# Attention and two feed-forward blocks in one kernel: other SBUF places for the matmul operands, a later normalisation, another prologue

## The chip, the core and the metric

One core of a Trainium2 chip runs the whole program. TensorE (PE, with its weight loads PEld), VectorE (DVE), ScalarE (ACT), GpSimd (POOL) and SyncE (SP) run side by side, each through its own instructions in order; they wait for each other on semaphores. SBUF is the working memory (128 partitions), PSUM holds what TensorE adds up. The metric is device time in microseconds (us).

## The reference

```python
x = attention(q, k, v, cap)              # 2 x 12 heads, 448 positions, head size 64
#   s = cap * tanh(q k^T / 8 / cap);  p = exp(s - max);  p v / (sum p + 1e-9)
x = x.transpose(0, 2, 1, 3).reshape(896, 768)
y = ((x @ w_a) * (x @ w_b)) @ w_out      # 768 -> 1536 -> 768
h = relu(y @ w_in)
out = (h * h) @ w_out2                   # 768 -> 2048 -> 768
```

The weights come in double precision, all else in single; the output is single.

## The kernel before

**Prologue.** Queries and keys of head pair 0, the number `cap`, pair 1 (`qk1`, into the third raw weight buffer) and the first unit of weights are loaded (lines 525 to 530). Eight matmuls on a small constant `warm` keep TensorE busy meanwhile. Then come the scores of pair 0, three DVE instructions that turn `cap` into the factor `c1`, and the tanh of pair 0 on ScalarE (lines 541 to 549).

**Attention.** A loop over 12 head pairs; one pass is a period. In a period `j`, TensorE computes the scores of pair `j+1` (`qk_main`, L52), their last 64 rows (`tails`, L58, into the PSUM tile `dn`), the products with `v` (L251, L286) and the column sums (L292, L294). ScalarE does tanh and exp. DVE adds up exp values (`presum`, L279 and L280), copies the results out of PSUM (`evac`: `ev` L298, `dv` L301) and normalises older pairs: `dv` goes through DMA into a shape with more partitions (`s8`, L304), is inverted (`recips`), written to DRAM (`dscr`, L328) and read back as a broadcast `rb` (`spread`, L335); `norm` (L342) multiplies `ev` by `rb`. `xhi` and `xlo` split the result into the two parts (high and low) that the products below take. `dv` has one buffer, and `dn` one bank: the next `tails` waits until `dv` has read `dn`.

**Weights.** A unit is six blocks of 128 x 128 weights (68 units). `conv(u, step)` turns the double-precision raw data of unit `u` into two parts in seven steps, which end in one of four buffers `whl0` to `whl3` (unit `u` uses number `u mod 4`). Steps 6 (L122 or L124) and 7 (L129) write the buffer. During attention the steps are spread over the periods by the table `CONV_AT`.

**Products.** `mm` (L184) multiplies a block with an operand tile: high part of the weights times low part of the operand (L189), low times high (L191), high times high (L193), each for two halves of 448 columns, so that a block is six matmuls and a unit 36, of one weight load (128 columns) and 448 streamed columns each. The operands are `x`, `g`, `y` and `h` (its last tile is `hlast`), one after another through the four matrix products; there are 2448 such matmuls, and a unit's weights are made three units ahead.

**Places.** In the built program the byte address in a partition, modulo 256, of each buffer's first byte in use is the following (`placed`, `HLAT` and the filler tiles set it; within a tile all parts lie at multiples of 256 bytes from its start, so a tile has one remainder):

| operand tiles | remainder | distance from `whl0` (at 0) | `whl1` (32) | `whl2` (64) | `whl3` (128) |
|---|---|---|---|---|---|
| `x` | 0 | 0 | 224 | 192 | 128 |
| `g` | 160 | 160 | 128 | 96 | 32 |
| `y` | 96 | 96 | 64 | 32 | 224 |
| `h` (tile at 224, data 48 bytes in) | 16 | 16 | 240 | 208 | 144 |
| `hlast` | 0 | 0 | 224 | 192 | 128 |

The distance is that of the operand behind the weights, modulo 256.

Of the kernel before, what the change touches and what calls it, by code (L numbers as in the profile page):

```python
# [37 lines left out]
HLAT = (0, 32, 64, 128)  # L38
# [9 lines left out]
def score(nc, banks, qk):  # L48
    for n in range(2 * NC):
        c, i = divmod(n, 2)  # L50
        r = slice(i * D, (i + 1) * D)
        nc.tensor.matmul(banks[n // NC][:, n % NC, :S], lhsT=qk[r, 1, c * P:(c + 1) * P], rhs=qk[r, 0], start=True, stop=True)  # L52


def score_tail(nc, out, qk):
    for i in range(2):
        r = slice(i * D, (i + 1) * D)
        nc.tensor.matmul(out[r, :S], lhsT=qk[r, 1, NM:], rhs=qk[r, 0], start=True, stop=True)  # L58
# [11 lines left out]
def placed(pool, name, n, gap, lead=0, room=0):  # L70
    if gap:
        pool.tile([P, gap // 4], F32, name=f"{name}gap")
    size = 2 * B * S
    tiles = [pool.tile([P, size + room // 4], F32R, name=f"{name}{i}")[:, lead // 4:lead // 4 + size] for i in range(n)]
    return [t.rearrange("p (t b s) -> p t b s", t=2, b=B) for t in tiles]


def body(ctx, tc, qk, v, wu, out, c1, cabs, guard, dscr, qk1, kept, bounded):
# [17 lines left out]
    cur = 0  # L96
    whl = []
    for i, a in enumerate(HLAT):
        if a - cur:
            wp.tile([P, (a - cur) // 4], F32, name=f"whlgap{i}")  # L100
        whl.append(wp.tile([P, 2, UC], F32R, name=f"whl{i}"))
        cur = a
# [98 lines left out]
    xhl = placed(xpool, "x", KD, 128)  # L201
# [35 lines left out]
    def qk_main(j):  # L237
        th = tht[j] = ap.tile([P, NT, S], F32, tag="th", name="th", bufs=1)
        sc = [ps.tile([P, NC, 512], F32, tag="sc", name="sc") for _ in range(2)]
        score(nc, sc, qkt[j])  # L240
# [3 lines left out]
    def tails(j):  # L244
        pvt[j] = pq[0].tile([P, 512], F32, tag="pv", name="pv")
        dnt[j] = pq[0].tile([P, 512], F32, tag="dn", name="dn")
        if j + 1 < NPAIR:
            score_tail(nc, dnt[j], qkt.pop(j + 1))
# [47 lines left out]
    def evac(j):  # L296
        ev = ap.tile([P, S], F32, tag="ev", name="ev", bufs=5)
# [9 lines left out]
    def finish(j):  # L307
# [8 lines left out]
        rb = ap.tile([P, S], F32, tag="rb", name="rb", bufs=2)  # L316
# [13 lines left out]
    def spread(j):  # L330
        if j < 0:
            return
        rb = ap.tile([P, S], F32, tag="rb", name="rb", bufs=2)
# [27 lines left out]
    for n in range(7):  # L361
        conv(0, n + 1, True)
# [15 lines left out]
    for j in range(last):  # L378
        qk_main(j + 1)
        presum(j)  # L380
        if j > 0:
# [7 lines left out]
        xhi(j - 4)  # L389
        xlo(j - 4)  # L390
        steps(j)
        norm(j - 3)
# [5 lines left out]
    spread(last - 2)  # L398
    xhi(last - 4)
# [38 lines left out]
    ghl = placed(gp, "g", NF1, 0)  # L438
    gp.tile([P, 16], F32, name="gback")
# [16 lines left out]
    yhl = placed(yp, "y", KD, 224)  # L456
# [10 lines left out]
    hhl = placed(hpool, "h", NF2 - 1, 0, 48, 256)  # L467
# [38 lines left out]
def tile_kernel(ctx, tc, qk, v, cap, wu, out):  # L506
# [12 lines left out]
    h_last = keep.tile([P, 2, B, S], F32R, name="hlast")  # L519
# [3 lines left out]
    with tc.manual_schedule():  # L523
        craw, cabs, c1, small, eps = (cp.tile([P, 1], F32, name=n) for n in ("craw", "cabs", "c1", "small", "eps"))
        qk0 = wk.tile([P, 2, S], F32, name="qk0")
# [85 lines left out]
```

## Time and profile before

| | |
|---|---|
| median of 3 runs | 599.25 us (598.66 to 599.28) |
| the profiled execution: its time | 599.35 us |
| its span, first to last instruction | 597.2 us |
| TensorE busy, share of the span | 585.3 us, 98% |
| VectorE busy | 389.8 us, 65% |
| ScalarE busy | 239.8 us, 40% |
| mean granted TensorE clock | 0.999 |

The profile is one execution. A busy TensorE row is a modelled span of pipelined matmuls, so its pace is read from start times, not from durations. All times below count from the first instruction; the time of the run has 2.15 us more than the span.

### The profile page before, as it was taken

How to read it: one execution, taken by the hardware profiler on the slowest of the kernel's cores; microseconds unless marked ns; L12 is line 12 of the kernel's file. 1: busy time of each engine (PE TensorE's matmuls, PEld its weight loads, DVE VectorE, ACT ScalarE, POOL GpSimd, SP SyncE). 2: the span in 40 equal slices, each digit the busy share in tenths (PEclk: the TensorE clock that was granted, in tenths of full speed). 3: DMA queues.
4: the chain of work that ended last, by engine and by line, in shares of the span. 5: the costliest groups of instructions: out<-in, count | busy, mean ns of one | idle time of the engine just before them, and what ended most of it. 6: DMA issues, size and time to landing. Idle time of an engine off the chain costs nothing.

```text
span 597.2 us, 7213 instructions
## 1 busy us (share of the span) xinstructions
PE 585.3 (98%) x2936; PEld 488.0 (82%) x2936; DVE 389.8 (65%) x525; ACT 239.8 (40%) x250; POOL 0.3 (0%) x5
## 2 busy tenths in 40 slices
PE   8899899999999999999999999999999999999996
PEld 2233236999999999999999999999999999999995
DVE  3778788788666666657555548787877686526400
ACT  6899790344333333322222224444444433212200
POOL 0000000000000000000000000000000000000000
PEclk9999999999999999999999999999999999999999
DMA  7455431244333333332333332332332335323001
GB/s 244 158 166 168 136 113 67 93 159 156 112 112 111 105 106 105 107 107 77 134 105 106 106 105 95 113 110 106 106 106 106 105 107 190 136 85 107 31 32 36
DMA packets 20549, 67.68 MB, mean 113 GB/s; under 512 B 6044, under 2 KB 9756, under 8 KB 20508
## 3 DMA queue, kind: packets, MB, share of 16 engines
q1 hardware_dynamic: 19356, 62.75, 31.0%
q10 hardware_dynamic: 1152, 4.39, 2.2%
q8 instruction: 25, 0.41, 0.3%
q14 instruction: 16, 0.13, 0.1%
HBM read 64.26 MB, written 2.79 MB: 112 GB/s over the span
## 4 chain that ended last, share of the span: by engine, by line
PE 93%; DMA 3%; DVE 2%; SPq 0%; issue 0%; ACT 0%; DVEq 0%
PE sc L189 19%; PE sc L191 19%; PE sc L193 19%; PE pd L193 9%; PE pd L191 9%; PE pd L189 9%; PE pv L286 4%; PE sc L52 3%; DMA raw<-in_wu_dram 1%; PE dn L292 1%; PE dn L58 1%; DMA s<-dv 1%; DMA dscr<-rc 1%; DMA rb<-dscr 0%; DVE sm L280 0%; DVE sm L279 0%
## 5 line engine op out<-in xcount | busy, mean ns | idle before, releaser
L124 ACT ACTIVATE whl<-nar 128x768 fp32r<-128x768 f32 x65 | 55.1, 847 | 181.7 <-DVE nar L149 154.8
L129 DVE TENSOR_TENSOR whl<-nar,whl 128x768 fp32r<-128x768 f32 x68 | 65.1, 958 | 40.0 <-ACT whl L124 40.0
L147 DVE SCALAR_TENSOR_TENSOR nar<-raw,nar 128x768 int32<-128x768 int32 x68 | 65.2, 958 | 2.3
L149 DVE SCALAR_TENSOR_TENSOR nar<-raw,nar 128x768 int32<-128x768 int32 x68 | 64.9, 955 | 1.4
L141 ACT ACTIVATE nar<-nar 128x768 f32<-128x768 f32 x65 | 54.3, 835 | 20.9 <-DVE nar L134 20.9
L189 PE MATMUL sc<-x,whl 128*128 128x448 f32 x192 | 56.7, 366 | 0.0
L191 PE MATMUL sc<-x,whl 128*128 128x448 f32 x192 | 56.6, 365 | 0.0
L193 PE MATMUL sc<-x,whl 128*128 128x448 f32 x192 | 56.6, 366 | 0.0
L145 DVE TENSOR_SCALAR nar<-nar 128x768 int32<-128x768 int32 x68 | 37.6, 552 | 18.0 <-ACT nar L141 17.6
L134 DVE TENSOR_SCALAR nar<-raw 128x768 f32<-128x768 f32 x68 | 37.6, 553 | 3.4 <-DMA raw<-in_wu_dram 3.4
L189 PEld LDWEIGHTS sc<-x,whl 128*128 128x128 f32 x192 | 36.0, 188 | 4.4 <-issue 1.4
L193 PEld LDWEIGHTS sc<-x,whl 128*128 128x128 f32 x192 | 36.0, 188 | 3.1
L191 PEld LDWEIGHTS sc<-x,whl 128*128 128x128 f32 x192 | 36.0, 188 | 3.0
L189 PE MATMUL sc<-y,whl 128*128 128x448 f32 x132 | 37.6, 366 | 0.0
L191 PE MATMUL sc<-y,whl 128*128 128x448 f32 x132 | 37.6, 365 | 0.0
L193 PE MATMUL sc<-y,whl 128*128 128x448 f32 x132 | 37.5, 365 | 0.0
L193 PE MATMUL sc<-h,whl 128*128 128x448 f32 x120 | 36.6, 366 | 0.0
L189 PE MATMUL sc<-h,whl 128*128 128x448 f32 x120 | 36.6, 366 | 0.0
L191 PE MATMUL sc<-h,whl 128*128 128x448 f32 x120 | 36.6, 366 | 0.0
L273 ACT ACTIVATE pe<-th,cabs 128x3136 f32<-128x3136 f32 x12 | 34.9, 2910 | 0.4
L242 ACT ACTIVATE th<-sc,c 128x1344 f32<-128x1344 f32 x22 | 29.1, 1375 | 7.7 <-PE sc L52 7.7
L286 PE MATMUL pv<-pe,vt 128*64 128x448 f32 x144 | 29.7, 548 | 0.0
(126 smaller groups left out, 996.9 us busy)
## 6 DMA issues: line engine op xcount, KB each, us to landing
raw<-in_wu_dram SPq DMA_DIRECT2D x63, 768.0 KB, 4.2
qk<-in_qk_dram SPq DMA_DIRECT2D x10, 448.0 KB, 4.4
raw<-in_wu_dram ACTq DMA_DIRECT2D x5, 768.0 KB, 5.5
vt<-in_v_dram SPq DMA_DIRECT2D x12, 224.0 KB, 4.6
rb<-dscr SPq DMA_DIRECT2D x22, 112.0 KB, 2.8
out_dram<-th SPq DMA_DIRECT2D x5, 448.0 KB
raw<-in_qk_dram SPq DMA_DIRECT2D x1, 448.0 KB, 6.5
s<-dv SPq DMA_DIRECT2D x22, 3.5 KB
```

The costliest lines, as they stand in the source:

```text
L124: nc.scalar.activation(out=hl[:, 0], in_=nar_t[u], func=AF.Copy)
L129: nc.vector.tensor_tensor(out=hl[:, 1], in0=nar_t.pop(u), in1=f32(hl[:, 0]), op=ALU.subtract)
L134: nc.vector.tensor_scalar(out=t, in0=raw_t[u][:, :, 1].bitcast(F32), scalar1=WTOP, scalar2=-WTOP, op0=ALU.min, op1=ALU.max)
L141: nc.scalar.activation(out=t, in_=t, func=AF.Copy, scale=2.0 ** -112)
L145: nc.vector.tensor_scalar(out=t, in0=t, scalar1=3, scalar2=None, op0=ALU.logical_shift_left)
L147: nc.vector.scalar_tensor_tensor(out=t, in0=r[:, :, 0], scalar=29, in1=t, op0=ALU.logical_shift_right, op1=ALU.bitwise_or)
L149: nc.vector.scalar_tensor_tensor(out=t, in0=r[:, :, 1], scalar=-(1 << 31), in1=t, op0=ALU.bitwise_and, op1=ALU.bitwise_or)
L189: nc.tensor.matmul(o[:, b, :S], lhsT=hi, rhs=m[:, 1, b], start=first, stop=False)
L191: nc.tensor.matmul(o[:, b, :S], lhsT=lo, rhs=m[:, 0, b], start=False, stop=False)
L193: nc.tensor.matmul(o[:, b, :S], lhsT=hi, rhs=m[:, 0, b], start=False, stop=last)
L273: nc.scalar.activation(out=pe, in_=th, func=AF.Exp, scale=cabs)
L286: nc.tensor.matmul(pvt[j][(1 - i) * D:(2 - i) * D, :S], lhsT=vt[:, n], rhs=pe[:, n], start=False, stop=c == NC - 1)
```

## The change

Four things change. (1) The four weight buffers lie at remainder 0, and every operand tile (`x`, `g`, `y`, `h`, `hlast`) at remainder 160: one distance, 160 bytes modulo 256, for all 2448 matmuls. `HLAT` goes, and `placed` takes filler before and behind instead. (2) In the attention loop `xhi`, `xlo` and `norm` work on a pair that is one period older; `ev` and `rb` get one more buffer each, and the set that falls out of the loop stands behind it. (3) Steps 6 and 7 of unit 0 are done behind the first `presum` instead of ahead of the first exp. (4) In the prologue `cap` is loaded by GpSimd's queue, the keys of pair 0 in two pieces, the first unit of weights by ScalarE's queue; the scores go to three PSUM tiles instead of two, and the tanh in three pieces behind them.

```diff
-HLAT = (0, 32, 64, 128)
...
-def placed(pool, name, n, gap, lead=0, room=0):
-    if gap:
-        pool.tile([P, gap // 4], F32, name=f"{name}gap")
-    size = 2 * B * S
-    tiles = [pool.tile([P, size + room // 4], F32R, name=f"{name}{i}")[:, lead // 4:lead // 4 + size] for i in range(n)]
-    return [t.rearrange("p (t b s) -> p t b s", t=2, b=B) for t in tiles]
+def placed(pool, name, n, before=0, behind=0):
+    if before:
+        pool.tile([P, before // 4], F32, name=f"{name}before")
+    tiles = [pool.tile([P, 2, B, S], F32R, name=f"{name}{i}") for i in range(n)]
+    if behind:
+        pool.tile([P, behind // 4], F32, name=f"{name}behind")
+    return tiles
...
-    cur = 0
-    whl = []
-    for i, a in enumerate(HLAT):
-        if a - cur:
-            wp.tile([P, (a - cur) // 4], F32, name=f"whlgap{i}")
-        whl.append(wp.tile([P, 2, UC], F32R, name=f"whl{i}"))
-        cur = a
+    whl = [wp.tile([P, 2, UC], F32R, name=f"whl{i}") for i in range(HLB)]
...
-    xhl = placed(xpool, "x", KD, 128)
+    xhl = placed(xpool, "x", KD, before=160)
...
-        ev = ap.tile([P, S], F32, tag="ev", name="ev", bufs=5)
+        ev = ap.tile([P, S], F32, tag="ev", name="ev", bufs=6)
...
-        rb = ap.tile([P, S], F32, tag="rb", name="rb", bufs=2)
+        rb = ap.tile([P, S], F32, tag="rb", name="rb", bufs=3)
...
-    for n in range(7):
+    for n in range(5):
...
+        if j == 0:
+            conv(0, 6, True)
+            conv(0, 7, True)
...
-        xhi(j - 4)
-        xlo(j - 4)
+        xhi(j - 5)
+        xlo(j - 5)
         steps(j)
-        norm(j - 3)
+        norm(j - 4)
...
+    xhi(last - 5)
+    xlo(last - 5)
+    norm(last - 4)
...
-    ghl = placed(gp, "g", NF1, 0)
-    gp.tile([P, 16], F32, name="gback")
+    ghl = placed(gp, "g", NF1, behind=64)
...
-    yhl = placed(yp, "y", KD, 224)
+    yhl = placed(yp, "y", KD, before=160)
...
-    hhl = placed(hpool, "h", NF2 - 1, 0, 48, 256)
+    hhl = placed(hpool, "h", NF2 - 1, behind=64)
...
-    h_last = keep.tile([P, 2, B, S], F32R, name="hlast")
+    h_last = placed(keep, "hlast", 1, before=160, behind=96)[0]
...
-        qk0 = wk.tile([P, 2, S], F32, name="qk0")
-        nc.sync.dma_start(out=qk0[:, 0], in_=qk[0, :, 0])
-        nc.scalar.dma_start(out=qk0[:, 1], in_=qk[0, :, 1])
-        nc.sync.dma_start(out=craw, in_=cap.broadcast_to([P, 1]))
+        q0, ka, kb = (wk.tile([P, n], F32, name=m) for n, m in ((S, "q0"), (P, "ka"), (S - P, "kb")))
+        nc.gpsimd.dma_start(out=craw, in_=cap.broadcast_to([P, 1]))
+        nc.sync.dma_start(out=q0, in_=qk[0, :, 0])
+        nc.scalar.dma_start(out=ka, in_=qk[0, :, 1, :P])
+        nc.scalar.dma_start(out=kb, in_=qk[0, :, 1, P:])
         nc.sync.dma_start(out=qk1, in_=qk[1])
-        fetch(nc.sync, raws, wu, 0)
+        fetch(nc.scalar, raws, wu, 0)
...
-        sc = [wps.tile([P, NC, 512], F32, tag="sc", name="sc") for _ in range(2)]
+        sc = [wps.tile([P, 2, 512], F32, name=f"sc{c}", bufs=1) for c in range(NC)]
...
-        score(nc, sc, qk0)
-        score_tail(nc, tl, qk0)
-        for part in range(2):
-            nc.scalar.activation(out=th0[:, part * NC:(part + 1) * NC], in_=sc[part][:, :, :S], func=AF.Tanh, scale=c1)
+        k0 = [ka] + key_blocks(kb, P)
+        score(nc, [t[:, n, :S] for t in sc for n in range(2)], q0, k0)
+        score_tail(nc, tl, q0, k0[NC])
+        for c in range(NC):
+            nc.scalar.activation(out=th0[:, 2 * c:2 * c + 2], in_=sc[c][:, :, :S], func=AF.Tanh, scale=c1)
```

On DVE, at pair 0, before (rows of unit 0's conversion, `presum` of pair 0, unit 1's first steps):

```order
L147 SCALAR_TENSOR_TENSOR nar_171<-raw0_66,nar_171 128x768
L149 SCALAR_TENSOR_TENSOR nar_171<-raw0_66,nar_171 128x768
L122 CAST whl0_145<-nar_171 128x768
L129 TENSOR_TENSOR whl0_145<-nar_171,whl0_145 128x768
L556 TENSOR_SCALAR small_81<-small_81 128x1
L279 TENSOR_TENSOR sm_206<-pe_179 128x896
L280 TENSOR_TENSOR sm_206<-sm_206,pe_179 128x896
L134 TENSOR_SCALAR nar_219<-raw1_67 128x768
L139 TENSOR_SCALAR nar_219<-nar_219 128x768
```

and now:

```order
L145 SCALAR_TENSOR_TENSOR nar_175<-raw0_66,nar_175 128x768
L147 SCALAR_TENSOR_TENSOR nar_175<-raw0_66,nar_175 128x768
L562 TENSOR_SCALAR small_83<-small_83 128x1
L278 TENSOR_TENSOR sm_208<-pe_181 128x896
L279 TENSOR_TENSOR sm_208<-sm_208,pe_181 128x896
L120 CAST whl0_152<-nar_175 128x768
L127 TENSOR_TENSOR whl0_152<-nar_175,whl0_152 128x768
L132 TENSOR_SCALAR nar_223<-raw1_67 128x768
L137 TENSOR_SCALAR nar_223<-nar_223 128x768
```

The two steps that write `whl0` stand behind the two additions of `presum`, directly ahead of the first step on `raw1`.

On DVE, in period 6, before (the split of pair 2, two steps of unit 2, then `norm` of pair 3):

```order
L349 CAST x2_158<-xn_487 128x448
L355 TENSOR_TENSOR x2_158<-xn_487,x2_158 128x448
L139 TENSOR_SCALAR nar_485<-nar_485 128x768
L145 TENSOR_SCALAR nar_485<-nar_485 128x768
L342 TENSOR_TENSOR xn_545<-ev_385,rb_479 128x448
L298 COPY ev_557<-pv_525 128x448
L301 COPY dv_559<-dn_526 128x448
```

and now:

```order
L348 CAST x1_161<-xn_487 128x448
L354 TENSOR_TENSOR x1_161<-xn_487,x1_161 128x448
L137 TENSOR_SCALAR nar_485<-nar_485 128x768
L143 TENSOR_SCALAR nar_485<-nar_485 128x768
L341 TENSOR_TENSOR xn_545<-ev_335,rb_425 128x448
L297 COPY ev_557<-pv_525 128x448
L300 COPY dv_559<-dn_526 128x448
```

Ahead of the two copies of `evac` there now stands the product of pair 2, with an `rb` that was asked for a period earlier.

On ScalarE's queue, at the start, before:

```order
L527 DMA qk_83<-in_qk_dram 128x448
L535 ACT_TABLE_LOAD
L535 ACTIVATE small<-eps 128x1
L548 ACTIVATE th_65<-sc,c_80 128x1344 x2
L549 ACTIVATE th_65<-tl,c_80 128x448
```

and now:

```order
L532 DMA ka<-in_qk_dram 128x128
L533 DMA kb<-in_qk_dram 128x320
L69 DMA raw_66<-in_wu_dram 128x1536
L540 ACT_TABLE_LOAD
L540 ACTIVATE small<-eps 128x1
L554 ACTIVATE th_65<-sc_98,c_82 128x896
L554 ACTIVATE th_65<-sc_99,c_82 128x896
L554 ACTIVATE th_65<-sc_100,c_82 128x896
L555 ACTIVATE th_65<-tl,c_82 128x448
```

The load of the first unit of weights (`raw_66`) came to this queue from SP's, behind the two pieces of the keys, and the tanh of the first six score blocks is three instructions of 896 columns.

## Rows read from the trace of the kernel before

**Rows 1.** Windows: us; busy us (count) of PE, PEld, DVE, ACT, POOL; clock; DMA.

```profile
310.00:430.00 120.00, 120.00 (x590) 110.50 (x590) 82.52 (x102) 45.99 (x54) 0.00 (x0) 1.00 0.30 103
```

**Rows 2.** Timeline, TensorE, ends of the product stretch: start us, us, instruction.

```profile
97.10 0.47 PE L189 MATMUL sc<-x,whl 128*128 128x448 f32 x1
...
591.73 0.36 PE L193 MATMUL sc<-hlast,whl 128*128 128x448 f32 x1
```

**Rows 3.** Timeline, TensorE, `x` products: first matmuls of five units.

```profile
115.48 0.57 PE L189 MATMUL sc<-x,whl 128*128 128x448 f32 x2
...
122.82 0.36 PE L189 MATMUL sc<-x,whl 128*128 128x448 f32 x1
...
130.12 0.57 PE L189 MATMUL pd<-x,whl 128*128 128x448 f32 x2
...
152.10 0.37 PE L189 MATMUL pd<-x,whl 128*128 128x448 f32 x1
...
159.53 0.36 PE L189 MATMUL sc<-x,whl 128*128 128x448 f32 x1
```

**Rows 4.** Timeline, TensorE, `g` products: three unit starts, one unit's end.

```profile
269.45 0.57 PE L189 MATMUL sc<-g,whl 128*128 128x448 f32 x2
...
276.25 0.57 PE L193 MATMUL sc<-g,whl 128*128 128x448 f32 x2
276.66 0.57 PE L189 MATMUL sc<-g,whl 128*128 128x448 f32 x2
...
284.01 0.36 PE L189 MATMUL sc<-g,whl 128*128 128x448 f32 x1
...
291.39 0.37 PE L189 MATMUL sc<-g,whl 128*128 128x448 f32 x1
```

**Rows 5.** Timeline, TensorE, `y` products: first matmuls of three units.

```profile
357.35 0.57 PE L189 MATMUL sc<-y,whl 128*128 128x448 f32 x2
...
364.74 0.56 PE L189 MATMUL sc<-y,whl 128*128 128x448 f32 x2
...
371.94 0.58 PE L189 MATMUL pd<-y,whl 128*128 128x448 f32 x2
```

**Rows 6.** Timeline, prologue and pair 0: start us, us, instruction, [idle, who ended it].

```profile
0.89 3.59 PE L539 MATMUL wacc<-warm 128*128 128x512 bf16 x8 [0.89 <-POOL warm L533]
...
1.18 0.42 SPq L528 DMA_DIRECT2D craw<-in_cap_dram  x1
...
6.07 0.16 DVE L541 SCALAR_TENSOR_TENSOR cabs<-craw 128x1 f32<-128x1 f32 x1 [5.20 <-DMA craw<-in_cap_dram]
...
7.26 0.97 PE L58 MATMUL tl<-qk 64*64 64x448 f32 x4
...
9.92 2.91 ACT L273 ACTIVATE pe<-th,cabs 128x3136 f32<-128x3136 f32 x1
...
10.14 0.60 DVE L134 TENSOR_SCALAR nar<-raw 128x768 f32<-128x768 f32 x1 [2.43 <-DMA raw<-in_wu_dram]
...
13.95 0.56 DVE L122 CAST whl<-nar 128x768 fp32r<-128x768 f32 x1
...
15.49 1.08 DVE L279 TENSOR_TENSOR sm<-pe 128x896 f32<-128x896 f32 x1
...
17.84 0.57 PE L292 MATMUL dn<-sm,ones 128*32 128x448 f32 x2 [1.58 <-DVE sm L280]
...
18.68 0.56 DVE L134 TENSOR_SCALAR nar<-raw 128x768 f32<-128x768 f32 x1 [0.99 <-DMA raw<-in_wu_dram]
```

**Rows 7.** Chain of work that ended last, around 58 us: start us, us, what.

```profile
57.84 4.81 DMA s<-dv
```

**Rows 8.** Timeline around 60 us, columns as in rows 6.

```profile
62.23 0.62 DVE L342 TENSOR_TENSOR xn<-ev,rb 128x448 f32<-128x448 f32 x1 [3.29 <-DMA rb<-dscr]
...
63.30 0.61 DVE L301 COPY dv<-dn 128x448 f32<-128x448 f32 x1
...
63.97 0.59 PE L58 MATMUL dn<-qk 64*64 64x448 f32 x2 [2.63 <-DVE dv L301]
```

More of the change, by code (lines that the diff above doesn't have):

```diff
@@ L45, in f32, with score @@
     return ap.bitcast(F32)
-def score(nc, banks, qk):
+def score(nc, outs, q, ks):
     for n in range(2 * NC):
@@ L51, in score, with score_tail, key_blocks @@
         r = slice(i * D, (i + 1) * D)
-        nc.tensor.matmul(banks[n // NC][:, n % NC, :S], lhsT=qk[r, 1, c * P:(c + 1) * P], rhs=qk[r, 0], start=True, stop=True)
-def score_tail(nc, out, qk):
+        nc.tensor.matmul(outs[n], lhsT=ks[c][r], rhs=q[r], start=True, stop=True)
+def score_tail(nc, out, q, k):
     for i in range(2):
         r = slice(i * D, (i + 1) * D)
-        nc.tensor.matmul(out[r, :S], lhsT=qk[r, 1, NM:], rhs=qk[r, 0], start=True, stop=True)
+        nc.tensor.matmul(out[r, :S], lhsT=k[r], rhs=q[r], start=True, stop=True)
+def key_blocks(k, first=0):
+    return [k[:, c * P - first:(c + 1) * P - first] for c in range(first // P, NC)] + [k[:, NM - first:]]
 def fetch(eng, raws, wu, u):
@@ L239, in qk_main @@
         sc = [ps.tile([P, NC, 512], F32, tag="sc", name="sc") for _ in range(2)]
-        score(nc, sc, qkt[j])
+        score(nc, [t[:, n, :S] for t in sc for n in range(NC)], qkt[j][:, 0], key_blocks(qkt[j][:, 1]))
         for part in range(2):
@@ L247, in tails @@
         if j + 1 < NPAIR:
-            score_tail(nc, dnt[j], qkt.pop(j + 1))
+            t = qkt.pop(j + 1)
+            score_tail(nc, dnt[j], t[:, 0], t[:, 1, NM:])
         for i in range(2):
@@ L332, in spread @@
             return
-        rb = ap.tile([P, S], F32, tag="rb", name="rb", bufs=2)
+        rb = ap.tile([P, S], F32, tag="rb", name="rb", bufs=3)
         for i in range(2):
```

## The prediction

> **What bounds it now.** I read the stretches first, then TensorE's start times, then the waits of the attention loop and the prologue. In the products TensorE has no idle moment (120.00 of 120 us, at clock 1.00), while DVE is busy 82.52 us of the 120, ScalarE 45.99 [rows 1]. So in this part only TensorE's own pace counts. Its busy time doesn't tell that pace; start times do. Its long stretch goes from 97.10 to 591.73 us [rows 2], and in it start 2430 of the 2448 product matmuls (the first 18 come earlier): 494.63 / 2429 = 203.6 ns each. That is 83% of the span. All of them are alike (one load of 128 columns, 448 streamed), at the full clock, and yet units of 36 don't take the same time, which is the first thing the reader should see:
>
> - `x` with `whl3` (distance 128): 115.48 to 122.82, 7.34 us. With `whl0` (distance 0): 122.82 to 130.12, 7.30 us; the same pair of buffers later 152.10 to 159.53, 7.43 us [rows 3].
> - `g` with `whl0` (160): 269.45 to 276.66, 7.21 us; with `whl1` (128): 7.35; with `whl2` (96): 284.01 to 291.39, 7.38 [rows 4].
> - `y` with `whl0` (96): 357.35 to 364.74, 7.39; with `whl1` (64): 7.20 [rows 5].
>
> The order of these numbers goes with the distance, not with the product or the buffer: 128 gives 7.34 and 7.35 in two products with two buffers, 96 gives 7.38 and 7.39. Nothing waits for another engine there, so what differs must be how the weight load of the next matmul and the stream of the present one meet in SBUF.
>
> **Term 1, the places.** All 2448 matmuls get the distance 160, and remainders (0 and 160) that the unit at 269.45 already has. Inside that unit 34 matmuls lie between 269.45 and 276.25 [rows 4]: 6.80 / 34 = 200.0 ns; start to start, with the step into the next unit, 7.21 / 36 = 200.3. After the change the next unit has the same distance, so the step should be no dearer. Bounds of the gain: 2429 x (203.64 - 200.3) = 8.1 us and 2429 x (203.64 - 200.0) = 8.8 us. I take **8.5 us**. The cover for it: DVE needs 82.52 / 120 = 69% of the time now and 70% at the new pace, and the code it runs there is the same.
>
> Here a rule speaks against the whole term. The Trainium skill, "SBUF — State Buffer", section "Who interferes with whom", gives TensorE two read ports, one for the stream and one for the weight load, and says "PE and ACT never wait on anyone". By it places change nothing and this term is 0. The trace does not bear it out as far as it goes: same work, same clock, no wait, 7.20 to 7.43 us.
>
> **Term 2, prologue and pair 0.** What ends last before is DVE: the first unit of weights lands at 10.14, its seven steps run to 15.49, `presum` follows, and TensorE waits 1.58 us for it before the column sums at 17.84 [rows 6]. Three parts move.
>
> *ScalarE.* The tanh waits for `c1`, thus for `cap`, which lands at 6.07 behind the queries on SP's queue. Loaded first by GpSimd's queue it should land by about the time at which the scores start (the warm matmuls end at 0.89 + 3.59 = 4.48), and the tanh then follows the scores: the tail scores end at 7.26 + 0.97 = 8.23, and one tanh of 448 columns (an estimate: 0.65 us, from exp's 0.93 ns a column, 2.91 us for 3136, and some 0.2 us to start) gives exp at 8.9 instead of 9.92. Against it: GpSimd must now issue this DMA before it clears `warm`, and the eight warm matmuls wait for that. No GpSimd DMA is in the trace. The nearest row is SP's issue of the same DMA, 0.42 us. From below the price is nothing, from above, as an estimate, the whole 1.0 us that the tanh gains; I take 0.6 us, a little over SP's row. Exp at 9.5, its end at 9.5 + 2.91 = 12.4.
>
> *DVE.* The conversion's last two steps, 15.49 - 13.95 = 1.54 us, leave the path. The raw unit itself no longer queues behind `cap`: between 4.48 (the scores start, so queries and keys are there) and 6.07 that queue still had `cap` to deliver, 512 bytes. So the unit lands between 10.14 - 1.59 = 8.55 and 10.14; I take 9.2. Five steps (10.14 to 13.95, 3.81 us) lead to 13.0, `presum` (15.49 to 17.84, 2.35 us) to 15.4.
>
> *TensorE.* Its own work from the end of exp (9.92 + 2.91 = 12.83) to the sums, without the wait, is 17.84 - 1.58 - 12.83 = 3.43 us: 12.4 + 3.43 = 15.85. That is the later one, and 17.84 - 15.85 = 2.0 us is what pair 0 gains.
>
> What is late next: DVE's first step on the second unit waits for its load until 18.68 (0.99 us idle), and the copies `ev` and `dv` of pair 0, for which the next `tails` waits, are queued behind that step and the next. Now the two moved steps are queued ahead of it as well: 15.4 + 1.54 = 16.9, so they are hidden as long as the load lands later. If it still lands at 18.68, most of the 2.0 us is given back. Its issue stands on ScalarE's queue behind the scores of pair 1 and moves with them, and the queue's backlog is smaller by what the first unit gained; I take 0.4 us given back, so **1.6 us**. Bounds: 0 (load as late as now, or GpSimd costs all) and 2.6 (GpSimd costs nothing: exp at 8.9, pair 0 gains 2.6, nothing given back).
>
> **Term 3, the later `norm`.** There is one wait of TensorE in the loop, 2.63 us at 63.97 in front of `tails`, for `dv` [rows 8]. DVE had stood 3.29 us in `norm` (62.23), waiting for `rb`; `ev` and `dv` (63.30) are queued behind. Now `norm` takes an older `rb`, which was asked for 6.7 us earlier, so that wait goes. But `dv` has one buffer, still read by the DMA into `s8`, which runs from 57.84 to 57.84 + 4.81 = 62.65 [rows 7]; the change doesn't touch that DMA or what SP issues ahead of it. So `dv` moves from 63.30 to about 62.7, and TensorE gets **0.6 us** of the 2.63. Bounds: 0 and 2.63, the latter if the shifted start lets the DMA through sooner. The extra `xhi`, `xlo` and `norm` behind the loop are on DVE while TensorE does the first products and the last pair; I cost them at nothing. Without that cover they cost about 0.3 + 0.6 + 0.6 = 1.5 us.
>
> **Sum.** Against the profiled execution (599.35 us, 2.15 us of it outside the span): 8.5 + 1.6 + 0.6 = 10.7, so 588.65. That execution is 0.1 us over the median of 599.25; **588.6 us**.
>
> **The rivals.**
>
> - *A second pace at the same distance.* Distance 0 shows two, 7.30 and 7.43 us [rows 3], with the same buffers; how a unit is entered seems to decide. If 160 has such a second pace 0.13 / 36 = 3.6 ns higher and most units fall into it, term 1 is gone: about 596; with half of them 592. Against it: the one unit shown locks to 200.0 from its third matmul on, and every unit would be entered from the same distance.
> - *Places don't matter:* the 7.20 and 7.21 are then an accident of those stretches, and terms 2 and 3 alone give 597.15. The equal numbers at equal distances speak against it. This is what the page of the Trainium skill named above, "SBUF — State Buffer", would have.
> - *Prologue gives nothing:* 590.2. *The whole attention wait goes:* 586.6; with the best prologue and pace 585.3.
> - *Slower.* The pace belongs to the two places and not to their distance, and `x`, `y` or `h` at 160 meet the weights worse than now. The worst unit shown is 7.43 / 36 = 206.4 ns. At that pace all over: 2429 x (206.4 - 203.64) = 6.7 us lost, 599.35 + 6.7 - 2.2 = 603.8. It decides from the point where the mean pace exceeds 203.64 + 2200 / 2429 = 204.5 ns. The remainders 0 and 160 themselves stand in the `g` unit, which leaves it little room.
>
> **How the numbers follow.** The forecast case (full pace, prologue and loop near the values taken, 587.3 to 590.0) 0.60; full pace, but little or nothing from the prologue (590.0 to 592) 0.14; more than I take from loop or prologue (585.3 to 587.3) 0.12; second pace (592 to 597) 0.08; places don't matter (about 597) 0.03; slower 0.03. From 586.4 to 592.0 lie 0.60 + 0.14 + about half of 0.12 = 0.80. A measurement tells about 0.2% (1.2 us) from no change, so faster is below 598.05: 0.60 + 0.14 + 0.12 + 0.08 + 0.03 less a little = 0.95; within 0.2%: 0.02; slower 0.03.
>
> **What the profile afterwards would show.** Term 1: units of 36 product matmuls all take 7.20 to 7.21 us, in each of the four products; the product stretch lasts about 486 us instead of 494.6. Term 2: column sums of pair 0 at about 15.9 instead of 17.84; a GpSimd DMA row that tells its price, and the first warm matmul later by it. Term 3: no wait of DVE for `rb` in the loop, and a wait of about 2 us left in front of `tails` at pair 6, with the `s8` DMA as the last releaser. The prediction is wrong if units at distance 160 differ among themselves, or if a new wait for the second unit of weights eats the prologue's gain.

## The result, and the profile after

The changed kernel takes 591.76 us (median of four executions: 590.59, 592.18, 606.17, 591.34), the kernel before beside it 598.95; the ratio is 0.9873 (95% interval 0.9854 to 0.9893). Executions more than 1.5% above the fastest of their kernel are left out of all ratios here; what the one of 606.17 us probably is, the experiments tell. The profiled execution took 590.59 us, with a span of 588.4.

The products first: the timeline of TensorE in the changed kernel, first matmul of all, starts of units of each product, last matmul.

```profile
96.48 0.47 PE L187 MATMUL sc<-x,whl 128*128 128x448 f32 x1
...
107.39 0.36 PE L187 MATMUL pd<-x,whl 128*128 128x448 f32 x1
...
114.59 0.36 PE L187 MATMUL sc<-x,whl 128*128 128x448 f32 x1
...
265.79 0.36 PE L187 MATMUL sc<-g,whl 128*128 128x448 f32 x1
...
272.99 0.36 PE L187 MATMUL sc<-g,whl 128*128 128x448 f32 x1
...
352.19 0.36 PE L187 MATMUL sc<-y,whl 128*128 128x448 f32 x1
...
359.39 0.36 PE L187 MATMUL sc<-y,whl 128*128 128x448 f32 x1
...
582.39 0.36 PE L191 MATMUL sc<-hlast,whl 128*128 128x448 f32 x1
```

A unit takes 7.20 us in `x`, `g` and `y` alike, where it took 7.20 to 7.43 [rows 3 to 5]; 22 units of `x` lie between 107.39 and 265.79, (265.79 - 107.39) / (22 x 36) = 200.0 ns a matmul, the steps between units included. The stretch lasts 582.39 - 96.48 = 485.91 us instead of 494.63 [rows 2]: 8.72 us less. The window from 310 to 430 us (view and columns as in [rows 1]) holds 602 TensorE rows instead of 590:

```profile
310.00:430.00 120.00, 120.00 (x602) 112.61 (x601) 88.04 (x108) 48.04 (x58) 0.00 (x0) 1.00 0.31 106
```

Then the prologue and pair 0, which answer to [rows 6] (timeline of the changed kernel; in brackets the idle time and who ended it):

```profile
1.23 0.66 POOL L530 DMA_DIRECT2D craw<-in_cap_dram  x1 [0.78 <-POOLq L607]
...
1.88 0.12 POOL L538 MEMSET warm<- 128x1 bf16 x1
2.06 3.60 PE L544 MATMUL wacc<-warm 128*128 128x512 bf16 x8 [2.06 <-POOL warm L538]
...
5.58 1.87 PE L51 MATMUL sc<-q,ka 64*128 64x448 f32 x4
...
7.24 0.16 DVE L546 SCALAR_TENSOR_TENSOR cabs<-craw 128x1 f32<-128x1 f32 x1 [6.37 <-DMA craw<-in_cap_dram]
...
8.94 0.97 PE L57 MATMUL tl<-q,kb 64*64 64x448 f32 x4
...
10.01 0.56 DVE L132 TENSOR_SCALAR nar<-raw 128x768 f32<-128x768 f32 x1 [1.12 <-PE tl L57]
...
11.25 2.92 ACT L272 ACTIVATE pe<-th,cabs 128x3136 f32<-128x3136 f32 x1
...
13.85 0.33 ACTq L69 DMA_DIRECT2D raw<-in_wu_dram  x1
...
14.36 1.08 DVE L278 TENSOR_TENSOR sm<-pe 128x896 f32<-128x896 f32 x1
...
16.48 0.55 DVE L120 CAST whl<-nar 128x768 fp32r<-128x768 f32 x1
...
17.52 0.57 PE L291 MATMUL dn<-sm,ones 128*32 128x448 f32 x2
...
19.68 0.56 DVE L132 TENSOR_SCALAR nar<-raw 128x768 f32<-128x768 f32 x1 [1.65 <-DMA raw<-in_wu_dram]
...
21.28 0.61 DVE L300 COPY dv<-dn 128x448 f32<-128x448 f32 x1
...
21.95 0.59 PE L57 MATMUL dn<-qk 64*64 64x448 f32 x2 [1.01 <-DVE dv L300]
```

GpSimd issues `cap` first, and `warm` follows only at 1.88, so the warm matmuls start at 2.06 instead of 0.89 [rows 6]. `cap` itself lands later than before (7.24, not 6.07), exp starts at 11.25 instead of 9.92, and the sums of pair 0 stand at 17.52: 0.3 us earlier, not 2.0. Then DVE waits for the second unit until 19.68 (before 18.68), with `dv` queued behind it: the next `tails` start at 21.95, against 21.18 in the trace before. Between these two executions the prologue has lost 0.8 us (further profiles, below, scatter by about 1 us).

Last the loop, which answers to [rows 7] (chain of work that ended last) and [rows 8] (timeline):

```profile
57.84 4.61 DMA s<-dv
```

```profile
58.76 0.62 DVE L341 TENSOR_TENSOR xn<-ev,rb 128x448 f32<-128x448 f32 x1
...
62.57 0.62 DVE L300 COPY dv<-dn 128x448 f32<-128x448 f32 x1 [2.66 <-DMA s<-dv]
...
63.25 0.59 PE L57 MATMUL dn<-qk 64*64 64x448 f32 x2 [1.15 <-DVE dv L300]
```

`norm` no longer waits for `rb`; `dv` waits for the DMA into `s8` instead, TensorE 1.15 us instead of 2.63. The products begin 97.10 - 96.48 = 0.62 us earlier, prologue and loop taken together. Sum: 8.72 + 0.62, less 0.6 by which the end (last matmul to end of span) came out longer, is the 8.8 us between the two profiled executions (599.35 and 590.59).

### The profile page after: what moved, and what is told of

Read it like the earlier page. It is cut to its first block, busy times and chain, and to the rows that moved or that the text cites. A ratio compares the mean times of both kernels' runs of the same rounds, so it can differ in the third digit from the quotient of the medians.

```text
span 588.4 us, 7218 instructions
## 1 busy us (share of the span) xinstructions
PE 577.2 (98%) x2936; PEld 488.2 (83%) x2936; DVE 390.1 (66%) x525; ACT 240.3 (41%) x251; POOL 1.0 (0%) x6
## 4 chain that ended last, share of the span: by engine, by line
PE 94%; DMA 2%; ACT 1%; DVE 1%; issue 0%; POOL 0%; DVEq 0%; ACTq 0%; POOLq 0%; SPq 0%
PE sc L187 19%; PE sc L191 19%; PE sc L189 19%; PE pd L191 9%; PE pd L187 9%; PE pd L189 9%; PE pv L285 4%; PE sc L51 3%; PE dn L57 1%; PE dn L291 1%; DMA raw<-in_wu_dram 1%; ACT pe L272 1%; DMA s<-dv 1%; PE wacc L544 1%; ACT th L240 0%
## 5 line engine op out<-in xcount | busy, mean ns | idle before, releaser
L187 PE MATMUL sc<-x,whl 128*128 128x448 f32 x192 | 56.2, 364 | 0.0
L189 PE MATMUL sc<-x,whl 128*128 128x448 f32 x192 | 55.9, 362 | 0.0
L191 PE MATMUL sc<-x,whl 128*128 128x448 f32 x192 | 55.9, 362 | 0.0
L189 PE MATMUL sc<-y,whl 128*128 128x448 f32 x132 | 37.1, 362 | 0.0
L187 PE MATMUL sc<-y,whl 128*128 128x448 f32 x132 | 37.1, 362 | 0.0
L191 PE MATMUL sc<-y,whl 128*128 128x448 f32 x132 | 37.1, 362 | 0.0
L187 PE MATMUL sc<-h,whl 128*128 128x448 f32 x120 | 36.2, 362 | 0.0
L189 PE MATMUL sc<-h,whl 128*128 128x448 f32 x120 | 36.2, 362 | 0.0
L191 PE MATMUL sc<-h,whl 128*128 128x448 f32 x120 | 36.2, 362 | 0.0
```

The costliest lines, as they stand in the source:

```text
L187: nc.tensor.matmul(o[:, b, :S], lhsT=hi, rhs=m[:, 1, b], start=first, stop=False)
L189: nc.tensor.matmul(o[:, b, :S], lhsT=lo, rhs=m[:, 0, b], start=False, stop=False)
L191: nc.tensor.matmul(o[:, b, :S], lhsT=hi, rhs=m[:, 0, b], start=False, stop=last)
```

## The experiments

The table holds all kernels: ratio to executions of the kernel before taken beside it, with its interval, executions over 601.5 us, and from the profile of each when the first `tails` behind pair 0's sums start and when the product stretch begins.

| kernel | distances | ratio | over 601.5 us | tails | stretch |
|---|---|---|---|---|---|
| before | twelve | 1 | none | 21.18 | 97.10 |
| changed | 160 | 0.9873 (0.9854 to 0.9893) | 1 of 4 | 21.95 | 96.48 |
| `e1_places` | 160 | 0.9848 (0.9822 to 0.9873) | 1 of 4 | 20.99 | 98.92 |
| `e2_rest` | twelve | 0.9996 (0.9984 to 1.0008) | none | 21.08 | 95.44 |
| `e3_dv2` | 160 | 0.9896 (0.9876 to 0.9917) | 3 of 7 | 21.65 | 97.75 |
| `e4_mixed` | one in each product | one execution, 601.02 us | 0 of 1 | 21.71 | 97.50 |
| `e5b_oldpro` | 160 | 0.9848 (0.9818 to 0.9877) | 4 of 7 | 19.72 | 94.42 |
| `e6_rem` | 160 | one execution, 590.83 us | 0 of 1 | 20.93 | 97.01 |
| `e7_capact` | 160 | 0.9854 (0.9829 to 0.9880) | 1 of 6 | 20.80 | 98.55 |
| `e9_alt_dv2` | 160, 64 in turn | 0.9910 (0.9889 to 0.9932) | 0 of 6 | 21.89 | 101.64 |
| `e10_oldpro_alt` | 160, 64 in turn | 0.9854 (0.9830 to 0.9878) | 0 of 4 | 20.39 | 96.03 |
| `e11_oldpro_y64` | 160, `y` 64 | 0.9846 (0.9820 to 0.9872) | 2 of 6 | 20.41 | 97.16 |
| `e12_oldpro_d64` | 64 | 0.9851 (0.9827 to 0.9875) | 0 of 5 | 20.88 | 95.91 |
| `e13_keys2_alt` | 160, 64 in turn | 0.9852 (0.9827 to 0.9877) | 0 of 4 | 20.55 | 96.04 |

(Two executions stand alone and are left out: 726.16 us of `e2_rest` at a mean granted clock of 0.754, and 3313.07 us of `e7_capact`. There is no profile of either to explain it.)

**Places alone, and all but the places.** `e1_places` is the kernel before with the new `placed`, fillers and weight buffers; `e2_rest` is the changed kernel with the old ones:

```diff
-    xhl = placed(xpool, "x", KD, before=160)
+    xhl = placed(xpool, "x", KD, 128)
...
```

> The kernel before with the new places alone (weights at remainder 0, operands at 160). My theory (the pace goes with the distance): every unit of 36 product matmuls takes 7.20 us, the product stretch 486 us instead of 494.6, the attention loop stays as before with its 2.6 us wait at pair 6, and the time falls by 8.7 to about 590.6 us. Rival (the gain came from the order of work ahead of the products, or needs it): units at 7.2 to 7.4 us as before, about 599 us.

> The changed kernel with the old places: norm one period later, new prologue, unit 0's last two steps behind presum. My theory: product units as before (7.20 to 7.43 us), products begin at about 96.5 us instead of 97.1, time within 0.7 us of before, 598.3 to 599.5 us. Rival (the later norm and the new prologue bring something of their own that is lost in the changed kernel): 596 to 598 us.

The places alone give 599.25 x (1 - 0.9848) = 9.1 us (7.6 to 10.7), everything else together 0.2 us (-0.5 to 1.0). On top of the places the rest shows no gain either: 0.9873 for the changed kernel, 0.9848 for `e1_places`, with overlapping intervals. In `e2_rest` the units of `g` have their old lengths again (timeline of its TensorE, first matmuls of four units; distances 160, 128, 96):

```profile
267.79 0.37 PE L193 MATMUL sc<-g,whl 128*128 128x448 f32 x1
...
275.00 0.37 PE L193 MATMUL sc<-g,whl 128*128 128x448 f32 x1
...
282.35 0.36 PE L193 MATMUL sc<-g,whl 128*128 128x448 f32 x1
...
289.74 0.37 PE L193 MATMUL sc<-g,whl 128*128 128x448 f32 x1
```

7.21, 7.35 and 7.39 us, as in [rows 4]: neither the prologue nor the loop touches the products.

**Other distances, and the same distance elsewhere.** `e4_mixed` puts the operands at other remainders, the weights stay at 0: `x` at 96, `g` at 64, `y` at 128, `h` at 224.

```diff
-    xhl = placed(xpool, "x", KD, before=160)
+    xhl = placed(xpool, "x", KD, before=96)
-    ghl = placed(gp, "g", NF1, behind=64)
+    ghl = placed(gp, "g", NF1, behind=160)
-    yhl = placed(yp, "y", KD, before=160)
+    yhl = placed(yp, "y", KD, before=128)
...
```

> The changed kernel with one distance for each product, each taken from another product or buffer of the kernel before: x at 96, g at 64, y at 128, h at 224, the weights always at 0. My theory (the distance decides): units of 36 take 7.39 us in x, 7.20 in g, 7.34 in y and 7.36 in h, the product stretch is about 495 us and the time about 600 us. Rival (what counts is that all units of a product have one distance, whichever it is): 7.20 everywhere, about 590.6 us. Second rival (the product or the absolute place decides): paces that do not go with these four distances.

Timeline of its TensorE, start and end of one unit of each product:

```profile
167.83 0.37 PE L187 MATMUL sc<-x,whl 128*128 128x448 f32 x1
...
175.22 0.37 PE L187 MATMUL pd<-x,whl 128*128 128x448 f32 x1
...
292.92 0.36 PE L187 MATMUL sc<-g,whl 128*128 128x448 f32 x1
...
300.12 0.36 PE L187 MATMUL pd<-g,whl 128*128 128x448 f32 x1
...
394.43 0.36 PE L187 MATMUL pd<-y,whl 128*128 128x448 f32 x1
...
401.77 0.37 PE L187 MATMUL sc<-y,whl 128*128 128x448 f32 x1
...
482.57 0.37 PE L187 MATMUL sc<-h,whl 128*128 128x448 f32 x1
...
489.93 0.37 PE L187 MATMUL sc<-h,whl 128*128 128x448 f32 x1
```

7.39, 7.20, 7.34 and 7.36 us: distance 96 costs in `x` what it cost in `g` and `y` before, 64 is as good as 160, and one distance for a whole product gives nothing by itself (span 598.8 us). `e6_rem` keeps the distance and moves both sides, weights at 96 and operands at 0:

```diff
+    wp.tile([P, 24], F32, name="whlbefore")
     whl = [wp.tile([P, 2, UC], F32R, name=f"whl{i}") for i in range(HLB)]
...
-    h_last = placed(keep, "hlast", 1, before=160, behind=96)[0]
+    h_last = placed(keep, "hlast", 1)[0]
```

> The changed kernel with the weight buffers at remainder 96 and all operands at 0: the same distance 160 by other remainders. Theory (only the distance matters): every product matmul 200.0 ns (or all of them 206.7, if this execution falls into the second pace), span 588 to 590 (or 604 to 607). Rival (the remainders 0 and 160 matter themselves): some other pace, 202 to 206 ns, span 593 to 603 with differences between the products.

The window of [rows 1] in its trace:

```profile
310.00:430.00 120.00, 120.00 (x602) 112.61 (x601) 87.48 (x107) 48.33 (x57) 0.00 (x0) 1.00 0.31 106
```

All its product matmuls run at 200.0 ns, span 588.7. It is the distance, not the places (one execution; but each of its 66 whole units in the stretch took 7.20 us).

**A second `dv` buffer.** `e3_dv2`:

```diff
-        dv = ap.tile([P, S], F32, tag="dv", name="dv", bufs=1)
+        dv = ap.tile([P, S], F32, tag="dv", name="dv", bufs=2)
```

> The changed kernel with two buffers for dv. My theory (the wait that is left at pair 6 is dv waiting for the DMA that still reads its only buffer): DVE's wait for that DMA at 59.9 us (2.66 us) goes, TensorE's wait of 1.15 us in front of the tails of pair 6 falls below 0.3 us, and the products begin 0.8 to 1.2 us earlier, 589.5 us. Rival (that wait is the DMA queue itself being late, and something behind it, the load of pair data or the broadcast, waits next): the wait stays within 0.3 us of 1.15 or comes back at pair 7 to 9, no change.

The wait before the `tails` of pair 6 goes, but another of 2.18 us comes before the sums of the last pair: the later pairs' DMA chain through SP is no shorter (the last write to `dscr` is issued at 95.53 us, in the changed kernel at 94.94), so the wait has moved, not gone. The products of the stretch begin at 97.75, later than with one buffer, part of it by the low clock shown below. And its profiled execution took 608.82 us. The timeline and the windows of its trace show what happened there:

```profile
95.27 0.97 PE L311 MATMUL dn<-sm,ones 128*64 128x448 f32 x4 [2.18 <-DVE rc L325]
```

```profile
92.00:96.30 4.30, 2.12 (x12) 0.50 (x10) 3.33 (x7) 0.00 (x0) 0.00 (x0) 1.00 0.17 55
96.30:99.70 3.40, 3.40 (x9) 1.85 (x10) 3.33 (x5) 0.00 (x0) 0.00 (x0) 0.50 0.24 68
...
310.00:430.00 120.00, 120.00 (x582) 108.59 (x581) 81.29 (x100) 43.34 (x51) 0.00 (x0) 1.00 0.32 106
```

Behind that wait the granted clock is at its lower level (1.2 GHz) for 3.4 us, and once it is back at 2.4 GHz the window from 310 us holds 582 rows in 120 us where the changed kernel has 602: 120 / 582 = 206.2 ns; start to start the mean over the last 2420 matmuls is 206.67. That is a second pace at distance 160, at the full clock, from the stretch's start to its end. (206.67 - 200.0) x 2429 = 16.2 us, which is what separates the executions of 604 to 609 us from those of 589 to 595 (an execution like this is called caught below; three caught ones have a trace, here and in `e5b_oldpro` and `e7_capact`; the others, the 606.17 us at the top among them, are told by their time alone).

**What starts and what ends the second pace.** `e9_alt_dv2` is `e3_dv2` with the weight buffers at remainders 0, 96, 0, 96, so the distance alternates between 160 and 64:

```diff
+    whl = []
+    for i in range(HLB):
+        whl.append(wp.tile([P, 2, UC], F32R, name=f"whl{i}"))
+        wp.tile([P, 40 if i % 2 else 24], F32, name=f"whlback{i}")
```

> The changed kernel with two dv buffers (the version that had 606 to 609 us in three of its executions and in the profile, where all product matmuls stood at 206.7 ns) and with the second and fourth weight buffer 96 bytes on, so that the distance alternates from unit to unit between 160 and 64, which both have 200.0 ns. My theory: a uniform distance has a second pace, entered where the clock rises again and kept because nothing disturbs it; a new distance in every unit does. So all units run at 200.0 to 200.2 ns but at most one or two behind a rise of the clock, and none of the executions is over 600; median 590 to 593. Rival: the second pace belongs to the execution and not to the way in; then some executions still have 604 or more, and a profiled one that slow shows 206.7 in all units of distance 160.

None of its six executions is over 597 us, although its profiled one has the same low clock at the start of the stretch; units of distance 160 run at 200.0, those of 64 at 200.1 ns. (The profiled one took 596.18 us, since its stretch begins at 101.64: TensorE waited 1.48 us at 81.31 for a load of queries and keys, 3.43 us at 98.58 before the sums of the last pair, and the low clock followed. That the median of 594.5 has the same reason is not shown.) So a mixture of two good distances from unit to unit was never caught: none of 14 executions with `e10_oldpro_alt` and `e13_keys2_alt` below, while kernels with 160 alone were caught in 10 of 29; by chance that comes with (19/29)^14 = 0.003. `e11_oldpro_y64` asks whether the pace is drawn anew at each entry: distance 160 for `x`, `g` and `h`, 64 for `y` (on top of `e5b_oldpro`, below):

```diff
-    yhl = placed(yp, "y", KD, before=160)
+    yhl = placed(yp, "y", KD, before=64)
```

> As e5b_oldpro (uniform distance 160, four of seven executions at 604 to 608), but the operands y of the third product at distance 64. At 206.67 instead of 200.0 ns the x and g products cost 1295 x 6.67 = 8.6 us, the h products 575 x 6.67 = 3.8 us. My theory (the pace is drawn where a run of equal distances is entered, and lasts until another distance comes): the executions lie at 589, about 593, about 598 or about 602, and x and g on the one side and h on the other can differ; a profile shows each of them at 200.0 or 206.7 throughout. Rival (the pace belongs to the execution): only 589 and 602, and x, g and h always have the same pace.

The executions lie at 590.71, 591.63, 589.33, 590.29 and at 601.96, 603.6: nothing in between. The profiled one, 590.71, is not caught. My theory that each entry draws for itself had put some in between; the runs speak for the rival (`x`, `g` and `h` together: 8.6 + 3.8 = 12.4 us is what separates the two groups), though with two caught executions, neither with a trace, this isn't settled. If it holds, `h` was caught again although the units of `y` at 64 lie between. `e12_oldpro_d64` has 64 throughout, `g`, `y`, `h` and `hlast` like `x`:

```diff
-    xhl = placed(xpool, "x", KD, before=160)
+    xhl = placed(xpool, "x", KD, before=64)
...
```

> As e5b_oldpro with the uniform distance 64 in place of 160. Theory (the second pace belongs to distance 160, since 64 showed none in the kernel before and in e9_alt_dv2): all executions at 588.5 to 591, product matmuls at 200.06. Rival (any uniform distance has it): some of the executions 603 to 609, as with 160.

200.0 ns in all products, and five executions of 589.4 to 592.19 us. Five in a row without a caught one would come by chance with (19/29)^5 = 0.12, so a lower risk at 64 is likely and not shown.

**The prologue.** `e5b_oldpro` is the changed kernel with the old loads, scores and two tanh; the conversion's two steps stay behind `presum`. The core of the edit (the keys in one load, two PSUM tiles of scores and two tanh are left out):

```diff
-        nc.gpsimd.dma_start(out=craw, in_=cap.broadcast_to([P, 1]))
...
+        nc.sync.dma_start(out=craw, in_=cap.broadcast_to([P, 1]))
...
-        fetch(nc.scalar, raws, wu, 0)
+        fetch(nc.sync, raws, wu, 0)
...
```

> The changed kernel with the loads, scores and tanh of the prologue as they were (cap on SP's queue, keys in one load, two tanh); places, later norm and the new order of the conversion stay. My theory: the warm matmuls start at 0.9 again, the clock is full at about 5.2, the first tails come at 21.2 or up to 0.5 earlier (21.95 in the changed kernel), but the products begin at the same time within 0.2 us (96.5), because the wait before the tails of pair 6 is set by SP's chain and the DMA into s8; so the time is that of the changed kernel, 591.0 to 592.0. Rival: what the prologue gains goes through to the products, which then begin at 95.7 or earlier, and the time is 0.8 us or more below the changed kernel's.

Timeline of its prologue:

```profile
0.89 3.59 PE L543 MATMUL wacc<-warm 128*128 128x512 bf16 x8 [0.89 <-POOL warm L537]
...
5.77 0.16 DVE L545 SCALAR_TENSOR_TENSOR cabs<-craw 128x1 f32<-128x1 f32 x1 [4.91 <-DMA craw<-in_cap_dram]
...
9.89 2.91 ACT L272 ACTIVATE pe<-th,cabs 128x3136 f32<-128x3136 f32 x1
...
16.16 0.57 PE L291 MATMUL dn<-sm,ones 128*32 128x448 f32 x2
...
17.45 0.56 DVE L132 TENSOR_SCALAR nar<-raw 128x768 f32<-128x768 f32 x1 [0.72 <-DMA raw<-in_wu_dram]
...
19.72 0.59 PE L57 MATMUL dn<-qk 64*64 64x448 f32 x2
```

With the old loads the moved steps do what I had wanted of the whole: sums at 16.16, `tails` at 19.72. I had expected that the products would begin no earlier, because the DMA chain sets them; the stretch began at 94.42, 2.1 us before the changed kernel's. The chain of SP starts from pair 0's copies and moves with them (`s8` is issued at 55.12 there, at 57.23 in the changed kernel). So my theory fell: over the eight profiles with the later `norm`, one `dv` buffer and no low clock on the way, the stretch begins 74.4 to 76.1 us behind the first `tails`, so the start of pair 0 does go through to the products. But the scatter of 1.7 us is nearly as large as the effect, and 94.42 is the earliest of all: `e10_oldpro_alt` and `e12_oldpro_d64`, with the same prologue, begin at 96.03 and 95.91 (the first had been expected at 94 to 95, with `tails` at 19.5 to 20.2 and not at 20.39), while `e2_rest`, `e6_rem` and `e4_mixed`, with the changed kernel's prologue and loop, begin at 95.44, 97.01 and 97.50. On the mean the rival's direction holds; its 0.8 us in the time is not shown (the three executions not caught: 589.19 to 591.18 us, the intervals overlap).

This execution was also a caught one: 604.27 us, and 206.7 ns already in the 18 products that precede the last pair's attention, with no low clock since the prologue. The window of [rows 1] in its trace:

```profile
310.00:430.00 120.00, 120.00 (x583) 108.57 (x582) 80.91 (x100) 45.09 (x53) 0.00 (x0) 1.00 0.30 104
```

`e7_capact` leaves GpSimd out but keeps the rest of the new prologue; `cap` goes between the two pieces of the keys on ScalarE's queue:

```diff
-        nc.gpsimd.dma_start(out=craw, in_=cap.broadcast_to([P, 1]))
...
         nc.scalar.dma_start(out=ka, in_=qk[0, :, 1, :P])
+        nc.scalar.dma_start(out=craw, in_=cap.broadcast_to([P, 1]))
```

> The changed kernel with cap loaded on ScalarE's queue between the two pieces of the keys; nothing on GpSimd ahead of the warm memset. My theory: the warm matmuls start at 0.9, the clock is full at about 5.3, cap lands before 6.1, so exp starts at 10.0 to 10.4 (11.25 in the changed kernel) and pair 0's sums at 16.3 to 16.8 (17.52); but the load of the second unit is issued hardly earlier than 13, so the first tails come at 21.0 to 21.5 and not at 20, and the products begin at 96.5 as in the changed kernel. Time 591.0 to 592.0. Rival (GpSimd's price was the only fault of my sum): first tails at 20 or earlier, and 1 us or more less than the changed kernel.

`e13_keys2_alt` and `e10_oldpro_alt` then stand against each other: both with alternating distances and `cap` and unit 0 on SP's queue, the first with the keys in two pieces and three tanh, the second with the old ones. Of the first's edit the weight buffers, as in `e9_alt_dv2`, are not printed:

```diff
...
-        nc.gpsimd.dma_start(out=craw, in_=cap.broadcast_to([P, 1]))
         nc.sync.dma_start(out=q0, in_=qk[0, :, 0])
+        nc.sync.dma_start(out=craw, in_=cap.broadcast_to([P, 1]))
...
-        fetch(nc.scalar, raws, wu, 0)
+        fetch(nc.sync, raws, wu, 0)
```

> As e10_oldpro_alt, but with the keys in two pieces on ScalarE's queue and three tanh, as in the changed kernel; cap and the first unit of weights stay on SP's queue. Theory (the loss of the new prologue is GpSimd's late warm start, and the rest the longer queue of ScalarE with keys, and unit 0 behind them): first tails at 19.6 to 20.3, within 0.3 us of e10_oldpro_alt. Rival (the split of the keys is what costs): TensorE waits for the second piece in the scores, and the first tails are at 20.6 to 21, 0.8 us or more later than in e10_oldpro_alt.

> The changed kernel with the prologue's loads, scores and tanh as they were (as in e5b_oldpro) and the weight buffers alternating between remainder 0 and 96, so that the distance is 160 and 64 in turn. My theory: both gains add up: first tails at 19.5 to 20.2, products begin at 94 to 95, product matmuls at 200.0 to 200.1 ns, span 586 to 588.5, none of the executions over 600, median 588.5 to 590.5. Rival: the alternation costs something itself (e9_alt_dv2 had a median of 594.5), then the median is 592 or more; or the second pace comes here too, then some executions have 603 to 609.

Timeline of `e7_capact`, the second piece of the keys:

```profile
6.91 1.40 PE L51 MATMUL sc<-q,kb 64*128 64x448 f32 x6 [0.70 <-DMA kb<-in_qk_dram]
```

With `cap` ahead of it that piece comes late and TensorE waits 0.70 us in the scores; `tails` at 20.80, a little earlier than my theory had it (21.0 to 21.5) and not at 20, but the products began at 98.55 and not with the changed kernel's: TensorE waited 2.81 us at 63.76, and this execution has 3.4 us at the lower clock from 64.0 us on (it was also a caught one, 608.29 us; five others lie at 588.38 to 592.1). Without `cap` on that queue the split costs little: 20.55 in `e13_keys2_alt` against 20.39, and 590.32 against 590.59 us. The split was not the loss. Six profiles with `cap` on GpSimd's queue have `tails` at 20.93 to 21.95 (mean 21.54), six without it and with the new order of the conversion at 19.72 to 20.88 (mean 20.46): 1.1 us, about what the warm matmuls lose (1.17). The two with the old order and `cap` on SP's queue have 21.18 and 20.99, so by these means the order gives some 0.6 us and the change as a whole takes 0.45; with a scatter of about 1 us within each group neither is shown firmly. The values scatter, since the time at which the clock reaches its full level does, too: 4.22 to 6.88 us with the same start of the warm matmuls.

**The best version.** `e10_oldpro_alt`, `e12_oldpro_d64` and `e13_keys2_alt` lie at 590.59, 590.08 and 590.32 us, ratios 0.985, without an execution over 592.2. Against the changed kernel's other three executions (median 591.34) that is about 1 us, and the intervals overlap; what they do gain over it is that none of their 13 executions was caught. The 1 us is likely, not shown. For kernels with 160 alone the median hides the price: 10 of 29 executions took about 16.2 us more, 5.6 us a time on the average, more than half of what the places gain.

## Why the prediction was right or wrong

The time, 591.76 us, is 3.2 above the forecast of 588.6 and lies in the case of full pace and little or nothing from the prologue (590.0 to 592), not in the case that was given 0.60. Of the 591.76, 0.4 us is the caught execution in the median (591.34 without it). In the profiled pair, term 1 came, terms 2 and 3 together gave 0.62 of 2.2 us, and the end of the kernel, which no term had, took 0.6.

- **What bounds the kernel, and term 1.** Right. 8.72 us against 8.5 (bounds 8.1 to 8.8), and the places alone give the whole gain (`e1_places`). Reading the pace from start times and sorting it by distance was the step that carried it. The rule of the Trainium skill, "SBUF — State Buffer", section "Who interferes with whom", by which TensorE never waits for anyone and its two reads are independent, would have made term 1 nothing. For the other engines the traces agree, since TensorE has no idle moment in the products; but `e1_places` and `e2_rest` show that the places are worth 9.1 us, and by `e4_mixed` and `e6_rem` the pace goes with how its own two operands lie to each other. What happens between the two inside the chip no run shows.
- **Term 2** failed: 1.6 us of gain forecast, 0.8 lost at the `tails` of the profiled execution (over six profiles with this prologue 20.93 to 21.95, against 21.18 and 20.99 with the old one: no gain, and the loss within the scatter); with term 3 the two should give 2.2 us, and `e2_rest`, which has nothing else, gives 0.2 (-0.5 to 1.0). Four of its steps went wrong. The price of GpSimd's DMA: the row is 0.66 us, close to my 0.6, but the warm matmuls came 1.17 us later in all (2.06, not 0.89), because GpSimd issued the DMA only at 1.23 and `warm` had to follow. The landing of `cap`: I had it by about 4.5, since it was first in its queue. It landed at 7.24; the list of DMA issues gives 6.0 us from issue to landing:

```profile
craw<-in_cap_dram POOLq DMA_DIRECT2D x1, 0.5 KB, 6.0
```

  The second unit of weights on ScalarE's queue, 768 KB, took 5.8. SP's queue delivered `cap` at 6.07 [rows 6], and at 5.46 to 5.90 in other runs, GpSimd's at 6.67 to 7.24 in six: a queue of its own did not make it faster. (The Trainium skill, "DMA: Bandwidth & Descriptors", section "Anatomy of one DMA — SWDGE (gpsimd) path", fits a GpSimd transfer of this size at about 2.0 us. By it, as an estimate, `cap` would have been there at some 3.2 us. The trace, with 6.0 us, does not agree, and the measurement decides.) The first conversion step: I had it at 9.2 with the load of the first unit; it starts at 10.01, and what ended DVE's wait there is not the load but the tail scores of TensorE, late with the warm matmuls. And what is late next: the load of the second unit, which I had named, moved the wrong way, its issue from 12.52 to 13.85, its landing from 18.68 [rows 6] to 19.68; the prediction had named a new wait there as a sign of being wrong. The one step that held is the moved conversion: with exp at 9.89, `e5b_oldpro` has the sums at 16.16, where I had worked out 15.85 from an exp at 9.5.
- **Term 3.** Right in its mechanism: `norm` waits for nothing, and `dv` stands at 62.57 (forecast 62.7), behind the `s8` DMA as said. The wait left at the `tails` of pair 6 is 1.15 us, not the 2 I had named; 1.48 of it went. That the products begin 0.62 us earlier, where 0.6 was forecast, is luck: the 0.62 holds terms 2 and 3 together, and the prologue took its 0.8 out of what the loop gave. Better is the time from the first `tails` to the stretch: 75.92 us before, 74.53 in the changed kernel, and 75.2 on the mean of the eight profiles named above (74.4 to 76.1), so some 0.7 us for the term, with a scatter larger than that.
- **The rival "second pace at the same distance"** had a chance of 0.08 and a price of 3.6 ns, from the two paces of distance 0. It exists: 6.67 ns, in 10 of 29 executions with 160 alone, and in the three of them with a trace it lasts through the whole stretch, so an execution is either untouched or slower than the kernel before (604 to 609 us). The prediction's way to the price, 3.6 ns and a mixture of units in one execution, did not come. Its argument against the rival ("every unit would be entered from the same distance") did not protect the kernel; rather the kernels whose distance changes from unit to unit were never caught (14 executions). Whether the uniform distance is what holds the pace is not shown: in `e11_oldpro_y64`, by the times, `h` was caught behind units of another distance.
- **The rival "pair of places, not distance"** is out (`e4_mixed`, `e6_rem`), and so is "places don't matter".

Open stays what decides between the two paces. In `e3_dv2` the 18 products ahead of the low clock ran at 200.0 ns and all behind it at 206.67, which speaks for the moment at which the clock rises; in `e5b_oldpro` and `e7_capact` products on both sides of the last pair's attention ran at 206.7, with no rise of the clock between them, which fits. `e1_places` and `e11_oldpro_y64` had a low clock in the attention and 200.0 behind it, so a rise would have to draw the pace anew, either way; but then some execution of the alternating kernels should have shown 206.7 in its units of 160, about 8 us more. No run tells these apart.

## What to carry to other kernels

Where TensorE is the bound and never idle, read its pace from start times, sorted by the distance of the two operands modulo 256: here 160 and 64 gave 200.0 ns, others up to 206. Look at the highest times too, not only at the median: the kernels with one distance of 160 could keep a bad pace for the whole run, those with two good distances in turn did not. A small load does not come early by being first on a queue of its own; and what stands behind it on that engine (here the memset that starts the warm-up) is delayed by it.

## What the runs showed of the hardware that was not expected

- A stream of equal matmuls (128-column load, 448 streamed) at the full clock has two paces at distance 160, 200.0 and 206.67 ns, and kept either over the 2429 steps of the stretch (changed kernel, `e5b_oldpro`). Other distances have two paces within one execution: in the kernel before, units of 36 took 7.30 or 7.43 us at 0, 7.20 or 7.29 to 7.30 at 16, and 7.36 or 7.43 at 32.
- The granted clock falls to 1.2 GHz for 3.4 us behind some waits and not behind others: behind 2.54 us of waiting of TensorE in `e1_places`, 2.18 in `e3_dv2`, 1.87 in `e11_oldpro_y64`, not behind 2.63 in the kernel before. It cost 1.7 us in `e11_oldpro_y64`, where one period took 8.46 us (62.42 to 70.88) instead of 6.76.
- A load of 128 x 4 bytes took 6.0 us from GpSimd's queue with five larger loads issued between 0.74 and 1.66 us beside it.
